# Linear attention into a two-of-eight expert layer: the issue order written out by hand, numerator and denominator in one matmul, one expert begun early, rows transposed on TensorE

## The chip, the cores and the metric

The kernel runs on one core of a Trainium2 chip. The metric is the device time of one execution in microseconds. A core has a matrix engine (TensorE, PE in the profile, with its weight loads as PEld), a vector engine (VectorE, DVE), an activation engine (ScalarE, ACT), GpSimd (POOL), which here issues casting and indirect DMAs, and a sync engine (SP), which issues plain and transposing DMAs.

## The reference, cut to what matters

```python
def phi(x): return np.where(x > 0, x, np.exp(x) - 1.0) + 1.0
q_p, k_p = phi(q), phi(k)                    # 8 batches, 8 heads, 576 tokens, 64
kv  = np.einsum('bhsd,bhse->bhde', k_p, v)
z   = np.sum(k_p, axis=2)
x   = einsum(q_p, kv) / (einsum(q_p, z) + 1e-06)    # as 4608 tokens x 512
noisy = x @ w_gate + np.log1p(np.exp(x @ w_noise)) * noise
top2, top2_w = the two largest of 8, and the softmax of these two
for e in range(8):                           # w1: 512 x 1024, w2: 1024 x 512
    out[mask] += top2_w * (np.maximum(x[mask] @ w1[e], 0) @ w2[e])
```

## The kernel before, in words

**Attention** (class PhaseA) goes through four groups of two batches, 1152 tokens each. GpSimd loads q, k and v with a cast to bf16 (`load`). `phi` is one Exp on ScalarE and a max-add and a min on VectorE. `kv` multiplies keys with values; four extra heads of the value tile are all ones, so the key sums come out of the same matmul. It also multiplies the key-value product with the router weights (`wblk`), which gives 32 router columns beside the 128 numerator and 2 denominator columns of `kvbd`. `q_t` transposes phi(q) on TensorE. `group` then makes, for each three chunks of 128 tokens, the denominators and router columns (tile dl) in matmuls of 34 columns, and the numerators (tile num) in matmuls of 128 columns, and divides on VectorE into the row buffer xr. There are two row buffers, by turns of the group.

**Routing** (`route`) sums the router columns over heads, finds the top two experts, ranks every token within its expert with matmuls of triangular ones, and writes gate data into the row. Then 18 indirect DMAs a group (L358) scatter the rows of 1152 bytes into the DRAM array x_sorted, at the token's place among its expert's rows.

**Experts** (class PhaseB): every expert takes its first 1280 rows (CAP), in blocks of 512, 512 and 256. A transposing DMA (L496) brings a block as xt; `mm1` makes eight tiles of h, with Relu on ScalarE; `mm2` makes y for each 128 rows. The first visit of a token writes y, the second adds to what is there: `gather` brings the older output row into L by an indirect DMA (L438; skipped for first visits by an index out of bounds), VectorE forms gate times y plus L (L464), and an indirect DMA scatters it to the output (L465). The tails of one block (`mm2` and after) stand between the `mm1` parts of the next. Gathers depend on all earlier scatters to the output, since tokens of another expert may be the same. Rows beyond the capacity would be done by `overflow`, a loop at the end; with these inputs no expert has more than 1185 rows.

The framework's scheduler decides the order of instructions on each engine, from the dependencies and the order of the program. Rounds, by which experts could begin before attention ends (`early`), are there but the list ROUNDS is empty, so all experts begin after the last dispatch.

Of the kernel before, what the change touches and what calls it, by code (L numbers as in the profile page):

```python
# [15 lines left out]
P = 128  # L16
# [5 lines left out]

T_CAP = 10
CAP = T_CAP * P
E1 = 3

UNITS = [(0, 0, 9), (1, 0, 9), (2, 0, 9), (3, 0, 9)]

ROUNDS = []
# [3 lines left out]
KVW = 162  # L33
ACT_SET = "natural_log_exp_and_others"
# [11 lines left out]
def build_constants(tc, consts, w_gate, w_noise, noise):  # L46
    nc = tc.nc
    c = {}
    nc.scalar.preload_act_table_set(ACT_SET)

    ident = consts.tile([P, P], BF16, name="ident")
    nc.gpsimd.memset(ident[:], 0.0)
    nc.gpsimd.affine_select(
        out=ident[:], in_=ident[:], compare_op=ALU.not_equal, fill=1.0,
        base=0, pattern=[[-1, P]], channel_multiplier=1,
    )
    c["ident"] = ident

    ut = consts.tile([P, P], BF16, name="ut")
    nc.gpsimd.memset(ut[:], 0.0)  # L60
    nc.gpsimd.affine_select(
        out=ut[:], in_=ut[:], compare_op=ALU.is_ge, fill=1.0,
        base=0, pattern=[[-1, P]], channel_multiplier=1,
    )
    c["ut"] = ut

    ones = consts.tile([P, P], BF16, name="ones")
    nc.vector.memset(ones[:], 1.0)
    c["ones"] = ones


    c8 = consts.tile([P, E], FP32, name="c8")
    nc.gpsimd.iota(c8[:], pattern=[[-1, E]], base=E, channel_multiplier=0,
                   allow_small_or_imprecise_dtypes=True)
    nc.vector.tensor_scalar(out=c8[:], in0=c8[:], scalar1=1.0 / E, scalar2=None, op0=ALU.mult)
    c["c8"] = c8


    tokid = consts.tile([P, 9], FP32, name="tokid")
    nc.gpsimd.iota(tokid[:], pattern=[[1, 9]], base=0, channel_multiplier=9,  # L80
                   allow_small_or_imprecise_dtypes=True)
    c["tokid"] = tokid

    rowpos = consts.tile([P, T_CAP], FP32, name="rowpos")
    nc.gpsimd.iota(rowpos[:], pattern=[[P, T_CAP]], base=0, channel_multiplier=1,
                   allow_small_or_imprecise_dtypes=True)
    c["rowpos"] = rowpos

    mask = consts.tile([P, 130], FP32, name="mask")
    nc.vector.memset(mask[:], 0.0)  # L90
    nc.vector.memset(mask[0:64, 0:64], 1.0)
    nc.vector.memset(mask[0:64, 128:129], 1.0)
    nc.vector.memset(mask[64:P, 64:128], 1.0)
    nc.vector.memset(mask[64:P, 129:130], 1.0)
    c["mask"] = mask


    wst = consts.tile([P, 4, 16], FP32, name="wst")
    for half in range(2):
        for i, w in enumerate((w_gate, w_noise)):  # L100
            nc.scalar.dma_start(
                out=wst[64 * half : 64 * half + 64, :, 8 * i : 8 * i + 8],
                in_=w[256 * half : 256 * half + 256, :].rearrange("(a p) e -> p a e", p=64),
            )
    wblk = consts.tile([P, 4, 32], BF16, name="wblk")
    nc.vector.memset(wblk[:], 0.0)
    nc.vector.tensor_copy(out=wblk[0:64, :, 0:16], in_=wst[0:64])
    nc.vector.tensor_copy(out=wblk[64:P, :, 16:32], in_=wst[64:P])
    c["wblk"] = wblk

    noise_sb = consts.tile([P, 4, 9, E], FP32, name="noise_sb")
    for g in range(4):
        nc.scalar.dma_start(
            out=noise_sb[:, g], in_=noise[g * 2 * S : (g + 1) * 2 * S, :].rearrange("(p c) e -> p c e", c=9))
    c["noise"] = noise_sb

    carry = consts.tile([P, E], FP32, name="carry")
    nc.vector.memset(carry[:], 0.0)
    c["carry"] = carry
    c["cnt"] = [consts.tile([P, E], FP32, name=f"cnt{i}") for i in range(len(ROUNDS))]  # L120
    zero = consts.tile([P, 1], FP32, name="zero")
    nc.vector.memset(zero[:], 0.0)
    c["zero"] = zero
    return c


class PhaseA:


    def __init__(self, ctx, tc, q, k, v, x_sorted, c, psum):  # L130
        self.tc, self.nc, self.c = tc, tc.nc, c
        self.q, self.k, self.v, self.x_sorted = q, k, v, x_sorted
        self.ps_num, self.ps_dl, self.ps_misc = psum
        nc = tc.nc
        pool = lambda name, bufs: ctx.enter_context(tc.tile_pool(name=name, bufs=bufs, side="right"))
        self.kq = pool("A_kq", 3)
        self.pers = pool("A_pers", 1)
        self.ep = pool("A_e", 2)
        self.kvp = pool("A_kvp", 2)
        self.kvt = pool("A_kvt", 1)  # L140
        self.pq = pool("A_pq", 4)
        self.rt = pool("A_rt", 1)
        self.vt, self.xr = [], []
        for i in range(2):
            t = self.pers.tile([P, 12, S], BF16, name=f"v{i}")
            nc.vector.memset(t[:, 8:12, :], 1.0)
            self.vt.append(t)
        for i in range(2):
            t = self.pers.tile([P, 9, ROW_W], BF16, name=f"xr{i}")
            nc.vector.memset(t[:, :, HD:ROW_W], 0.0)  # L150
            self.xr.append(t)
        self.st = {}

    def load(self, g):
        nc = self.nc
        st = {}
        for t in "kvq":
            x = self.vt[g % 2] if t == "v" else self.kq.tile([P, 8, S], BF16, name="kq")
            for j in range(2):
                self.last_load = nc.gpsimd.dma_start(  # L160
                    out=x[64 * j : 64 * j + 64, 0:8, :],
                    in_=getattr(self, t)[2 * g + j].rearrange("h (p c) d -> p h (c d)", c=9)).ins
            st[t] = x
        self.st[g] = st

    def phi(self, x):

        nc = self.nc
        e = self.ep.tile([P, 4, 9, P], BF16, name="e")
        ev = lambda two: e[:, :, :, 64 * two : 64 * two + 64]  # L170
        xv = lambda two: x[:, 4 * two : 4 * two + 4, :].rearrange("p h (c d) -> p h c d", d=D)
        for two in range(2):
            nc.scalar.activation(out=ev(two), in_=xv(two), func=ACT.Exp)  # L173
        flat = x[:].rearrange("p a b -> p (a b)")
        nc.vector.tensor_scalar(out=flat, in0=flat, scalar1=0.0, scalar2=1.0, op0=ALU.max, op1=ALU.add)
        for two in range(2):
            nc.vector.tensor_tensor(out=ev(two), in0=ev(two), in1=xv(two), op=ALU.min)  # L177
        return e

    def kv(self, g, phk):  # L180
        nc, c = self.nc, self.c
        vt = self.vt[g % 2]
        kvbd = self.kvp.tile([P, 2, 4, KVW], BF16, name="kvbd")
        for h in range(2):
            ps = [self.ps_misc.tile([P, 2, 256], FP32, name="misc") for _ in range(2)]
            for i in range(2):
                hp = 2 * h + i
                for ci in range(9):
                    for j in range(2):
                        half = slice(64 * j, 64 * j + 64)  # L190
                        nc.tensor.matmul(  # L191
                            out=ps[j][:, i, 0:192], lhsT=phk[half, hp, ci, :],
                            rhs=vt[half, hp::4, 64 * ci : 64 * ci + 64],
                            start=(i == 0 and ci == 0), stop=(i == 1 and ci == 8), skip_group_check=True,
                        )
            for j in range(2):
                nc.vector.tensor_tensor(
                    out=kvbd[:, j, 2 * h : 2 * h + 2, 0:130], in0=ps[j][:, :, 0:130],
                    in1=_ap(c["mask"], [[0, 2], [1, 130]]), op=ALU.mult,
                )  # L200
        tp = self.ps_misc.tile([P, 1024], BF16, name="misc")
        for i in range(8):
            nc.tensor.transpose(tp[:, i * P : i * P + P], kvbd[:, i // 4, i % 4, 0:128], c["ident"][:])
        kvt = self.kvt.tile([P, 1024], BF16, name="kvt")
        nc.scalar.copy(out=kvt[:], in_=tp[:])
        wp = self.ps_misc.tile([P, 512], FP32, name="misc")
        for i in range(8):
            nc.tensor.matmul(
                out=wp[:, 32 * i : 32 * i + 32], lhsT=kvt[:, i * P : i * P + P], rhs=c["wblk"][:, i % 4, :],
                start=(i == 0), stop=(i == 7), skip_group_check=True,  # L210
            )
        nc.scalar.copy(out=_ap(kvbd, [[KVW, 8], [1, 32]], off=130), in_=wp[:, 0:256].rearrange("p (a b) -> p a b", a=8))  # L212
        return kvbd

    def q_t(self, phq, cs):

        nc = self.nc
        n = len(cs)
        pqt = self.pq.tile([P, 2, 4, P], BF16, name="pqt")
        tp = self.ps_misc.tile([P, 1024], BF16, name="misc")  # L220
        for i, ci in enumerate(cs):
            for hp in range(4):
# [148 lines left out]
class PhaseB:  # L371
# [35 lines left out]
    def meta(self, rows, nt, n_e, rowpos, code, group=None):  # L407
# [6 lines left out]
        if group:  # L414
            self.tc.add_to_no_dep_group(group, r.ins)
# [254 lines left out]
```

## Time and profile before

| | |
|---|---|
| time, median of 3 | 630.37 us (629.78 to 642.35) |
| span of the profiled run | 630.0 us, 6653 instructions |
| busy: PE / DVE / ACT / POOL | 376.8 / 204.0 / 162.1 / 265.9 us |
| matmuls of mm1 / mm2 | 768 / 640 |
| indirect DMAs: dispatch / gather / scatter | 72 / 70 / 80 |
| mean granted TensorE clock | 0.781 |

The span is what ends last; busy times of engines overlap. "Idle before, releaser" tells how long an engine stood still ahead of an instruction and what let it go on. The granted clock is the share of full speed that TensorE got.

### The profile page before, as it was taken

Reading aid. Unit: us, or ns where it says so; the run is one execution under the profiler, and the core shown is the slowest. Engines: PE = TensorE matmul, PEld = TensorE weight load, DVE = VectorE, ACT = ScalarE, POOL = GpSimd, SP = SyncE. Lnnn points to the kernel's source line nnn. Section 1 sums busy time; section 2 is a strip of 40 time slices with the busy share of each in tenths; the row PEclk is TensorE's granted clock in tenths of the full one; section 3 lists DMA queues with packets and bytes.
Section 4 is the critical chain, followed back from the end, with each engine's and each line's share of the span. In section 5 each row is a group of like instructions: output and inputs, shape, how many; then the busy total and the mean of one; then the engine's idle time right before and its main releaser. Section 6 shows DMA issues by size and latency. Waiting matters only on the chain. (4 is left out here: it accounts for less than half of the span.)

```text
span 630.0 us, 6653 instructions
## 1 busy us (share of the span) xinstructions
PE 376.8 (60%) x2520; PEld 204.8 (33%) x2520; DVE 204.0 (32%) x449; ACT 162.1 (26%) x257; POOL 265.9 (42%) x289
## 2 busy tenths in 40 slices
PE   0363634522441004493888997979979969789740
PEld 0352523412331001142334443443444434434410
DVE  4577447563027020021113333223432331333110
ACT  3460620710020002130322431422313314223200
POOL 5220683363720761043225454445445554443541
PEclk9975655755555556697779998997999989979985
DMA  9999939971310369979983443354354543554420
GB/s 147 207 218 249 225 109 195 210 198 53 117 48 1 119 117 199 201 129 184 118 104 111 125 111 116 84 123 125 75 138 141 147 109 101 157 150 119 133 88 18
DMA packets 97034, 83.77 MB, mean 133 GB/s; under 512 B 60469, under 2 KB 82997, under 8 KB 96992
## 3 DMA queue, kind: packets, MB, share of 16 engines
q0 software_dynamic: 40928, 69.90, 48.4%
q1 hardware_dynamic: 54400, 13.18, 13.4%
q10 hardware_dynamic: 1664, 0.18, 0.3%
q8 instruction: 21, 0.34, 0.2%
q14 instruction: 21, 0.17, 0.1%
HBM read 80.72 MB, written 33.95 MB: 182 GB/s over the span
## 5 line engine op out<-in xcount | busy, mean ns | idle before, releaser
L450 PE MATMUL h_ps<-xt,w 128*128 128x512 bf16 (+1 forms) x768 | 159.1, 355 | 67.8 <-DMA xt<-x_sorted 67.8
L458 PE MATMUL y_ps<-w,hT 128*128 128x512 bf16 x640 | 167.1, 409 | 33.2 <-DVE y L464 33.0
L452 ACT ACTIVATE hT<-h_ps 128x512 bf16<-128x512 f32 (+1 forms) x192 | 100.9, 526 | 299.4 <-PE h_ps L450 285.3
L465 POOL DMA_INDIRECT out_dram<-y,si x80 | 79.6, 996 | 123.1 <-DVE y L462 46.4
L450 PEld LDWEIGHTS <-w 128*128 128x128 bf16 x768 | 76.9, 100 | 144.6 <-issue 65.5
L358 POOL DMA_INDIRECT x_sorted<-xr,posi x72 | 72.8, 1011 | 84.0 <-issue 51.4
L464 DVE SCALAR_TENSOR_TENSOR y<-y_ps,gate,L 128x512 f32<-128x512 f32 x70 | 51.5, 737 | 173.3 <-DMA L<-out_dram,gi 108.5
L438 POOL DMA_INDIRECT L<-out_dram,gi x70 | 71.4, 1020 | 85.2 <-DMA out_dram<-y,si 66.5
L458 PEld LDWEIGHTS <-hT 128*128 128x128 bf16 x640 | 66.5, 104 | 115.5 <-issue 55.5
L435 DVE MEMSET L<- 128x512 f32 x70 | 34.0, 485 | 34.2 <-DMA x_sorted<-xr,posi 24.5
L173 ACT ACTIVATE e<-kq 128x2304 bf16<-128x2304 bf16 x16 | 33.5, 2122 | 27.6 <-PE misc L191 8.6
L191 PE MATMUL misc<-v,e 64*128 64x192 bf16 x288 | 24.4, 330 | 21.6 <-DVE e L177 19.9
L240 PE MATMUL num<-kvbd,pqt 128*64 128x128 bf16 x288 | 20.4, 283 | 26.4 <-DVE xr L259 25.9
L240 PEld LDWEIGHTS <-pqt 128*64 128x64 bf16 x576 | 21.8, 144 | 42.3 <-DVE xr L259 24.5
L191 PEld LDWEIGHTS <-e 64*128 64x128 bf16 x288 | 20.7, 123 | 24.1 <-DVE e L177 19.9
L309 PE MATMUL misc<-A,ut 128*128 128x72 bf16 x4 | 0.9, 217 | 44.6 <-DVE A L305 44.6
L259 DVE TENSOR_TENSOR xr<-num,rden 128x512 bf16<-128x512 f32 x36 | 23.5, 686 | 2.7 <-PE num L240 1.8
L225 ACT COPY pqt<-misc 128x1024 bf16<-128x1024 bf16 (+1 forms) x20 | 17.9, 932 | 17.2 <-remote 8.5
L224 PE MATMUL misc<-ident,e 128*128 128x128 bf16 x144 | 16.5, 291 | 9.7 <-ACT kvbd L212 4.5
L177 DVE TENSOR_TENSOR e<-e,kq 128x2304 bf16<-128x2304 bf16 x16 | 21.3, 1342 | 0.1
L403 POOL DMA_DIRECT2D w<-in_moe_w_dram x16 | 12.3, 778 | 17.4 <-DMA kq<-in_k_dram 8.3
L462 DVE TENSOR_SCALAR y<-y_ps,gate 128x512 f32<-128x512 f32 x10 | 7.3, 749 | 32.9 <-PE y_ps L458 28.6
(90 smaller groups left out, 157.8 us busy)
## 6 DMA issues: line engine op xcount, KB each, us to landing
w<-in_moe_w_dram POOLq DMA_DIRECT2D x32, 512.0 KB
kq<-in_k_dram POOLq DMA_DIRECT2D x8, 576.0 KB
v<-in_v_dram POOLq DMA_DIRECT2D x8, 576.0 KB
kq<-in_q_dram POOLq DMA_DIRECT2D x8, 576.0 KB
x_sorted<-zrow SPq DMA_DIRECT2D x16, 144.0 KB
out_dram<-y,si POOLq DMA_INDIRECT x80
x_sorted<-xr,posi POOLq DMA_INDIRECT x72
L<-out_dram,gi POOLq DMA_INDIRECT x70
```

The lines of the kernel that those rows point to most:

```text
L173: nc.scalar.activation(out=ev(two), in_=xv(two), func=ACT.Exp)
L191: nc.tensor.matmul(out=ps[j][:, i, 0:192], lhsT=phk[half, hp, ci, :], rhs=vt[half, hp::4, 64 * ci : 64 * ci + 64], start=(i == 0 and ci == ...
L240: nc.tensor.matmul(out=out[half], lhsT=pqt[ci][:, hp, half], rhs=kvbd[:, j, hp, cols], start=start, stop=stop, skip_group_check=True)
L259: nc.vector.tensor_tensor(out=_ap(xr[:, ci, 0:HD], [[64, 4], [256, 2], [1, 64]]), in0=_ap(ps, [[128, 4], [64, 2], [1, 64]]), in1=_ap(rden[ ...
L358: r = nc.gpsimd.indirect_dma_start(out=self.x_sorted, out_offset=bass.IndirectOffsetOnAxis(ap=posi[:, ci - c0, sl : sl + 1], axis=0), in_= ...
L435: nc.vector.memset(L[:], 0.0)
L438: nc.gpsimd.indirect_dma_start(out=L[:].bitcast(INT32), out_offset=None, in_=self.out.bitcast(INT32), in_offset=bass.IndirectOffsetOnAxis( ...
L450: nc.tensor.matmul(out=ps[:, 0:n], lhsT=w1[:, dc, fc * P : fc * P + P], rhs=xt[:, dc, 0:n], start=(dc == 0), stop=(dc == 3))
L452: nc.scalar.activation(out=hT[:, fc, 0:n], in_=ps[:, 0:n], func=ACT.Relu)
L458: nc.tensor.matmul(out=ps[:], lhsT=hT[:, fc, t * P : t * P + P], rhs=w2[:, fc, :], start=(fc == 0), stop=(fc == 7))
L464: nc.vector.scalar_tensor_tensor(out=y[:], in0=ps[:], scalar=gate, in1=L[:], op0=ALU.mult, op1=ALU.add)
L465: r = nc.gpsimd.indirect_dma_start(out=self.out, out_offset=bass.IndirectOffsetOnAxis(ap=si, axis=0), in_=y[:], in_offset=None, bounds_che ...
```

## The change

Nearly every function is rewritten; what is computed stays. Its parts:

- The scheduler is switched off (`manual_schedule`), and the order on all engines is that of the program. `attention` writes it out: in each of three loop turns the tail of group g is woven with the loads, phi and key-value product of group g + 1, and routing and dispatch of g come at the turn's end. The last group is routed and dispatched in two units of 6 and 3 chunks.
- Numerator, denominator and router columns come out of one matmul of 162 columns (`num`), into a tile of four PSUM banks with one buffer. The ones heads for the key sums are as before. The sum over heads is a tree of three adds.
- CAP is 1216, so blocks have 512, 512 and 192 rows.
- Expert 0 is begun early: its first 512 rows (dispatched after two groups) and next 256 (after three) are done while the last group is routed and dispatched.
- Rows of experts 1 to 7 are loaded untransposed and transposed on TensorE, with a copy on ScalarE (`xn_load`, `xn_t`). Only three blocks of expert 0 use the transposing DMA.
- Gathers and scatters of one expert are declared free of each other (group own). Each indirect DMA has a no-op on GpSimd ahead of it. L has 8 buffers and y has 8.
- `interval` orders a block: at a new expert the old expert's tails (t) come early and the gather at its end; within an expert the gather comes first. T is half of the next block's transposes.
- Weights of experts 0 and 1 are loaded during attention, those of e + 2 at the first block of e.

```diff
-T_CAP = 10
-CAP = T_CAP * P
-E1 = 3
-UNITS = [(0, 0, 9), (1, 0, 9), (2, 0, 9), (3, 0, 9)]
-ROUNDS = []
+CAP = 1216
+T_CAP = 10
+UNITS = [(0, 0, 9), (1, 0, 9), (2, 0, 9), (3, 0, 6), (3, 6, 9)]
+ROUNDS = [(1, 512), (2, 768)]
...
+    def num(self, g, t, *steps):
...
+            self.ps[g, t] = ps = self.ps_num.tile([P, 4, 512], FP32, name="num")
+            for hp in range(4):
+                for i in range(3):
+                    for j in range(2):
+                        half = slice(64 * j, 64 * j + 64)
+                        nc.tensor.matmul(
+                            out=ps[half, hp, KVW * i : KVW * i + KVW], lhsT=self.pqt[g, 3 * t + i][:, hp, half],
+                            rhs=self.kvbd[g][:, j, hp, :], start=(i == 0), stop=(i == 2), skip_group_check=True)
...
-        nc.vector.tensor_reduce(
-            out=lg, in_=_ap(self.lwt[:, c0], [[128, n], [1, 16], [16, 8]]), op=ALU.add, axis=AX.X)
+        for k in (4, 2):
+            nc.vector.tensor_tensor(out=lw(0, k), in0=lw(0, k), in1=lw(k, 2 * k), op=ALU.add)
...
-            r = nc.sync.dma_start(out=xt[:, :, 0:n], in_=self.x_sorted[r0 : r0 + n, 0 : HD // 2].bitcast(BF16),
-                                  transpose=True)
+    def xn_load(self, b):
...
+        nc.sync.dma_start(out=b["xn"][:, 0:k], in_=src(0, k * P).rearrange("(t p) d -> p t d", p=P))
...
+    def xn_t(self, b, h):
...
+            for dc in range(4):
+                nc.tensor.transpose(ps[:, i, dc, 0:m], b["xn"][0:m, t, dc * P : dc * P + P], self.c["ident"][0:m, 0:m])
...
+    def gather(self, b):
...
+            nc.gpsimd.nop()
+            r = nc.gpsimd.indirect_dma_start(
...
+            g = f"own{b['e']}"
+            tc.declare_no_dep(r.ins, group=g, reason="the rows of one expert are of distinct tokens")
+            tc.add_to_no_dep_group(g, r.ins)
...
+    def interval(self, cur, prev, weights=(), nxt=None):
...
+        if new:
+            steps = [0, "t", 1, "t", "t", "t", 2, 3, "T", 4, 5, "T", 6, 7]
         else:
+            steps = [0, 1, "t", 2, 3, "t", "T", 4, 5, "t", "T", 6, 7, "t"]
...
+    for g in range(3):
+        n = g + 1
+        pa.exp(n, "q")
+        pa.num(g, 0, 1)
+        pa.num(g, 1, 0)
+        pa.phi(n, "k")
...
+        if g == 1:
+            pa.dispatch(0, 6, 9)
+            pb.w_tiles(0)
+            pb.w_load(0, 0, 1, 2, 3)
+        pa.kv_mm(n, 0)
+        pa.num(g, 1, 1)
+        pa.num(g, 2, 0)
+        pa.kv_mm(n, 1)
...
+        pa.dispatch(g, 0, 6 if g == 0 else 9)
...
+    pb.mm1(r1, 3, 4, 5, 6, 7)
+    pb.meta("r1", c["cnt"][0][:], col[:, 0:4], code_of(0))
+    pb.interval(r2, r1)
...
+    with ExitStack() as order:
+        order.enter_context(tc.manual_schedule())
...
+        blocks = [pb.block(0, 768, CAP - 768, 0, 6, True)]
+        for e in range(1, E):
+            blocks += [pb.block(e, r, n, e, r // P) for r, n in ((0, 512), (512, 512), (1024, CAP - 1024))]
```

## The prediction

> **What bounds the kernel now.** I read four views. First the page's 40 slices (15.75 us each), for the stages:
>
> ```profile
> PE   0363634522441004493888997979979969789740
> ...
> POOL 5220683363720761043225454445445554443541
> PEclk9975655755555556697779998997999989979985
> DMA  9999939971310369979983443354354543554420
> ```
>
> TensorE is nearly full only from slice 20 (315 us) on. In slices 9 to 13 (142 to 220 us) neither TensorE nor the DMA engines have work. So the first half is bound by an order of waits and not by a resource. The stage table (window; busy us of PE, PEld, DVE, ACT, POOL, each with its count; granted clock; DMA share; GB/s) puts numbers on it:
>
> ```profile
> 0.00:62.00 62.00, 20.00 (x316) 16.87 (x318) 40.30 (x86) 24.72 (x22) 17.10 (x33) 0.79 1.13 204
> 62.00:140.00 78.00, 33.84 (x510) 28.03 (x509) 43.76 (x85) 28.63 (x27) 42.75 (x45) 0.59 0.93 189
> 140.00:227.00 87.00, 20.22 (x288) 16.71 (x288) 23.06 (x86) 7.91 (x16) 40.10 (x42) 0.52 0.21 73
> 227.00:245.00 18.00, 0.07 (x1) 0.07 (x1) 3.33 (x11) 0.00 (x0) 8.08 (x11) 0.50 1.02 155
> 245.00:323.00 78.00, 53.94 (x220) 23.50 (x220) 8.53 (x20) 18.60 (x34) 17.10 (x19) 0.78 1.14 162
> 323.00:365.00 42.00, 39.75 (x193) 19.15 (x192) 13.40 (x29) 13.62 (x26) 20.21 (x21) 0.96 0.41 104
> ```
>
> To 227 us it is attention and dispatch, in which VectorE, the busiest compute engine, works 107 of 227 us. 227 to 245 us TensorE does nothing: all experts wait for the last dispatched row. From 245 us it is experts. The waits (engine, tile, line, releaser: total us, times, longest) name what holds each stage:
>
> ```profile
> DVE y L464 <- DMA L<-out_dram,gi: 108.5, 23, 10.7
> PE h_ps L450 <- DMA xt<-x_sorted: 67.8, 4, 43.7
> POOL L L438 <- DMA out_dram<-y,si: 66.5, 20, 8.2
> PE y_ps L458 <- DVE y L464: 33.0, 12, 5.6
> ACT xr L340 <- DMA x_sorted<-xr,posi: 31.5, 2, 20.7
> ```
>
> The fifth is the stage of 140 us: a small ACT write into the row buffer waits 20.7 us for the dispatch of two groups earlier, and the router's Exp stands behind it. The second is the start of the experts, whose transposing load lands late. The other three are one chain in the expert stage: a gather waits for every earlier scatter, y waits for its gather, TensorE waits for the PSUM of y. The timeline shows the hand-over (start us, length, what):
>
> ```profile
> 225.07 0.96 POOL L358 DMA_INDIRECT x_sorted<-xr,posi  x1 [0.30 <-issue]
> ...
> 228.17 6.11 SPq L496 DMA_TRANSPOSE xt<-x_sorted  x1
> ```
> ```profile
> 244.93 8.53 PE L450 MATMUL h_ps<-xt,w 128*128 128x512 bf16 x32 [43.72 <-DMA xt<-x_sorted]
> ```
>
> In the steady part, 350 to 600 us, the line query counts 571 + 475 matmuls, 1046 in 250 us. An expert has 96 + 80 = 176, so it costs 42.1 us. Last, TensorE ends near 605 and the span at 630: a gather at 609 to 611, y, two scatters, and 13.7 us after the last scatter's issue.
>
> **What the Trainium skill says.** "TensorE: Matmul & The Clock Gate", section What's actually happening: 1.2 GHz when cold, 2.4 GHz after about 3.4 us of activity. The trace agrees: the first matmuls of 512 columns after a wait (from 245.31 us) are 0.43 us apart, later ones 0.216 us. So a TensorE wait costs its length and some 1.7 us more. Same page, Back-to-back issue gap: pairs of weight load and matmul with 128 columns run at about 81 ns; the trace has 16 transposes in 1.30 us at 73.30 us, 81 ns each. (Its 131 ns for 512 columns isn't seen here; I use 0.216.) "DMA: Bandwidth & Descriptors", section SWDGE vs HWDGE vs iDMA: GpSimd's and Sync's DMAs sit in different queues of the same 16 engines, which take turns. That fits the first xt, 16.8 us from issue to use while POOL issued weights.
>
> **The change, part by part.**
>
> *Attention in hand order.* The start to the first numerator stays: k and q land, phi, k'v, transposes; before reaches its first rden at 35.4 us, and I take 41 us, since the one matmul of 162 columns comes after the transposes of the whole group. Then each of three loop turns holds this VectorE work: phi of two tensors 2 x (1.36 + 2 x 1.34) = 8.1; three evacuations of 0.18 + 0.30 + 4 x 0.55 + 2 x 0.33 = 3.3, so 10.0 (the halves estimated from 686 ns for 512 columns and 548 ns for 384); key-value evacuation 4 x 0.42 = 1.7; tree sum in place of the 2.07 us reduce, about 1.4; routing 5.8 (149.25 to 155.0 us). Sum 27. Folding 288 denominator matmuls into the numerator takes 10.5 us of PE busy time away over the kernel, all beside VectorE: nothing on the path. The numerator has a single buffer of four PSUM banks, so TensorE now waits for its evacuation before the next one; on VectorE a phi stands in that gap, which hides it. I take 29 us a turn.
>
> *Dispatch.* 18 scatters at 1.27 us (spacing at 203 to 226 us) are 23 us a group, with loads under 30: below the VectorE turn or level with it. First dispatch at 41 + 29 = 70 us. From there POOL has 72 x 1.27 = 91 and ten issues of loads (the last q, two experts' weights) at 0.70 to 0.78, about 8: 169 us if never kept waiting. The ring does keep it waiting: before needed 116 to 147 us for a group with weight loads between, 8 us more than 23. I add 8, and 3 for landing: 180 us, against 227.
>
> *Early expert.* 768 rows of expert 0 (13.8 + 6.9 us of TensorE at 0.216) run while the last dispatch goes on: hidden by it. What is left waits for rows 768 to 1215 by transposing load: 16.8 us before, beside weights. Here the weights of expert 2 stand behind six scatters, so I take 10; bounds 6 (its issue) and 17. Start 190 us, against 245, and with one load in place of the four waits that drew the next 78 us out.
>
> *Expert work.* 1216 rows for 1280: first matmul 2 x 6.9 + 32 x 0.11 (192 columns, set by the weight load's 0.10) = 17.3; second 80 x 0.216 = 17.3 (the half tile still streams 512 columns); new: 38 transposes at 0.081 = 3.1. Sum 37.7 against 35.0 ideal before (13.8 + 3.9 + 17.3): the rows saved are eaten by transposes, which replace 20 transposing loads that are hidden once things run. The gain must come from the 7 us of waits in 42.1.
>
> *Gathers.* A gather no longer waits for scatters of its own expert, only at the first block of the next, and L has eight buffers in front. There the two tails of the old expert come early: last scatter at about 7 us of the interval, 3 to land (435.07 to 438.22 us), four gathers by 15.5, data 3 later, 18.5. Their y is wanted at 11.7 + 3.5 = 15.2 us. Four PSUM buffers for y hold 7 us of TensorE, so it is covered, narrowly. Behind these gathers stand four weight issues and the next gathers. POOL has 20 x 1.3 + 4 x 0.76 = 29 us an expert, below 37.7; the no-op ahead of each indirect DMA is unseen before: between 0 and 0.3 us (the gap there now); I take 0, the range keeps 6 us an expert, still hidden.
>
> *The sum.* From 190: rest of expert 0, 6.0 + two y tiles 3.5 + transposes 1.3 + cold start 2 = 12.8; its four y tiles 6.9; seven experts 7 x 37.7 = 264; waits 4%, 11 (the y margin is thin). TensorE ends at 485. Tail 16: y 0.75, two scatters, 13.7; no gather in it. **501 us.**
>
> **The rivals.** *Everything fits (12%).* No ring waits, a 6 us load, no waits in the experts: 169 + 3 + 6 + 12.8 + 6.9 + 264 + 15 = 477. For it: POOL and VectorE balance. *Attention is no shorter (15%).* In-order engines with a fixed order: one late wait holds all behind it. In 155 to 180 us the trace shows waits released by "remote", 14.9 and 8.1 us on ACT, long after TensorE's writes, while POOL dispatches; new dispatches lie beside all of attention. Rows at 227: 501 + 47 = 548. Against: before ran its first two groups beside dispatch with little of it. *Experts are no quicker (15%).* Gathers still come late behind weights, in the one GpSimd queue, so 42.1 stays and transposes come on top: 45.2 each, 7 x 7.5 = 52 less the 11: 542. Against: the profile's longest gather waits follow the scatter wait that goes. *POOL becomes the bound (5%).* If the no-op makes each indirect DMA wait for the one before, twice the spacing, 2.5 us each: 70 + 180 + 10 for dispatch, 7 x 53 for experts, 30 for the rest: 661, slower than before. [...] The forecast itself has 53%.
>
> **How the numbers follow.** 501 is the likeliest case. Half of 477's chance lies below 474; 548 is the upper rival. The range 474 to 550 leaves out the POOL case (5%), half of the first rival (6%) and the tails above the other two (7%). Faster by over 2% is below 618, which even both of these together (589) are: all but the POOL case, 95%. That one is slower (3%), or same (2%) where the no-op costs about two thirds of it.
>
> **What would show it.** Right: the last dispatch near 177 us, TensorE full from about 190, experts 37 to 40 us apart, the gather wait of VectorE under 30 us in total, no long wait on xt. Wrong: "remote" or dispatch waits in 70 to 170 us; VectorE waiting for gathers with TensorE cold in between; POOL busy through the expert stage.

## The result, and the profile after

The changed kernel takes **496.0 us** (median of 4, 494.9 to 497.4), the kernel before 630.1 us on the same chip: ratio **0.787, 95% interval 0.784 to 0.790** (medians here and below are over all runs, ratios leave out runs that lie well above the others of their kernel). The forecast was 501 us. These are the slices of the changed kernel's page that answer to those of before; a slice is now 12.3 us:

```profile
PE   0395354554332159999979999999997999999980
DVE  1928999695672102431351351351260342242330
POOL 6121258877667712437568547557467555546550
PEclk9997777666557559999998999999998999999995
DMA  9999993993974345395958846956956955434440
```

TensorE is full from slice 15 (185 us), where before it was slice 20 of 15.8 us (315 us). But look at slices 11 to 13: PE 3, 2, 1 and DVE 7, 2, 1, while POOL stands at 6, 7, 7. There the dispatch goes on and the early expert should run beside it. The stage table (columns as before: window, length, busy us with counts of PE, PEld, DVE, ACT, POOL, granted clock, DMA share, GB/s):

```profile
37.00:66.00 29.00, 14.81 (x209) 12.31 (x206) 25.68 (x69) 18.14 (x19) 4.67 (x7) 0.71 1.21 209
66.00:94.00 28.00, 15.11 (x215) 12.48 (x212) 23.80 (x64) 14.39 (x16) 22.82 (x22) 0.76 0.78 178
94.00:121.00 27.00, 12.75 (x168) 10.56 (x170) 22.62 (x53) 10.41 (x14) 20.60 (x20) 0.67 0.73 163
121.00:152.00 31.00, 12.84 (x111) 8.19 (x112) 20.59 (x89) 5.56 (x17) 21.50 (x24) 0.56 0.81 176
152.00:180.00 28.00, 6.05 (x14) 1.85 (x13) 3.21 (x23) 1.19 (x2) 18.19 (x19) 0.56 0.35 115
180.00:200.00 20.00, 18.08 (x88) 9.19 (x88) 4.13 (x16) 6.44 (x14) 3.92 (x4) 0.87 0.56 138
```

The first three rows are the loop turns, VectorE busy 23 to 26 us of each. In the fifth row (152 to 180 us) ScalarE completes 2 instructions in 28 us and VectorE 23. The timeline of that stretch (start us, length, instruction, in brackets the idle time before it and its releaser):

```profile
150.90 3.42 PE L512 MATMUL b<-xt,w 128*128 128x512 bf16 x8
164.57 1.87 PE L512 MATMUL b<-xt,w 128*128 128x512 bf16 x4 [10.25 <-issue]
175.07 1.86 PE L512 MATMUL b<-xt,w 128*128 128x512 bf16 x4 [8.63 <-issue]
180.70 4.97 PE L512 MATMUL b<-xt,w 128*128 128x512 bf16 x16 [3.77 <-ACT hT L514]
196.82 1.68 PE L512 MATMUL b<-xt,w 128*128 128x448 bf16 x8
...
163.92 0.60 ACT L514 ACTIVATE hT<-b 128x512 bf16<-128x512 f32 x1 [12.55 <-issue]
174.42 0.60 ACT L514 ACTIVATE hT<-b 128x512 bf16<-128x512 f32 x1 [9.90 <-remote]
180.06 1.08 ACT L514 ACTIVATE hT<-b 128x512 bf16<-128x512 f32 x2 [5.04 <-remote]
...
174.72 0.96 POOL L365 DMA_INDIRECT x_sorted<-xr,posi  x1 [0.30 <-issue]
180.51 1.62 SPq L446 DMA_TRANSPOSE xt<-x_sorted  x1
```

Four matmuls run every ten microseconds, and the trace names nothing that was waited for ("issue") or a source that it doesn't know ("remote"). I call this **the stop**. It ends 4 us after the last scatter has been issued; then the rest of the early rows runs, from 180.70 to 196.82 us, and the last rows of expert 0 (448 columns) begin at 196.82, though their load was issued at 180.51. The two names must be read with care. This trace has no landing time for any of the eight kinds of transfer that its page lists; the trace of the same program in the run after_third (below) has one for each. The weights on the two pages, and the same gather in the two timelines, each time the result's run first:

```profile
w<-in_moe_w_dram POOLq DMA_DIRECT2D x32, 512.0 KB
w<-in_moe_w_dram POOLq DMA_DIRECT2D x32, 512.0 KB, 8.5
258.47 1.05 POOL L495 DMA_INDIRECT L<-out_dram,gi  x1 [2.31 <-issue]
246.60 1.05 POOL L495 DMA_INDIRECT L<-out_dram,gi  x1 [2.31 <-DMA out_dram<-y,si]
```

The wait is 2.31 us long in both, and only the second trace names what ended it. So "issue" does not show here that an engine waited for nothing. That the engines stood still is in the start times. The waits that named the stages before:

```profile
DVE y L527 <- DMA L<-out_dram,gi: 14.8, 2, 8.0
POOL L L495 <- DMA out_dram<-y,si: 14.6, 5, 6.2
ACT hT L514 <- remote: 18.2, 5, 9.9
```

The gather wait of VectorE fell from 108.5 to 14.8 us and that of GpSimd's gathers from 66.5 to 14.6; the 67.8 us on xt is gone. (The page of the kernel before has no landing times either, so all these figures may be low; after_third has 18.0 and 18.9, and 22.1 on xt.)

### The profile page after: what moved, and what is told of

Its sections match the earlier page's. It is cut to its first block, busy times and chain, and to the rows that moved or that the text cites. A ratio compares the mean times of both kernels' runs of the same rounds, so it can differ in the third digit from the quotient of the medians.

```text
span 493.9 us, 6809 instructions
## 1 busy us (share of the span) xinstructions
PE 367.1 (74%) x2513; PEld 208.2 (42%) x2513; DVE 209.7 (42%) x526; ACT 187.0 (38%) x304; POOL 269.7 (55%) x289
## 4 chain that ended last, share of the span: by engine, by line
PE 62%; DVE 13%; DMA 10%; issue 4%; another core or an unknown queue 4%; ACT 4%; POOL 1%; POOLq 0%; ACTq 0%
PE b L512 29%; PE b L523 28%; DMA kq<-in_q_dram 7%; PE t L472 3%; DVE xr L254 3%; DMA x_sorted<-xr,posi 2%; DVE e L161 2%; ACT e L151 2%; PE num L243 1%; DVE kq L158 1%; DVE lwt L261 1%; DVE kvbd L192 1%; ACT hT L514 1%; PE misc L227 1%
## 5 line engine op out<-in xcount | busy, mean ns | idle before, releaser
L512 PE MATMUL b<-xt,w 128*128 128x512 bf16 (+3 forms) x768 | 158.1, 350 | 25.6 <-issue 19.3
L514 ACT ACTIVATE hT<-b 128x512 bf16<-128x512 f32 (+3 forms) x192 | 96.0, 510 | 163.2 <-PE b L512 110.4
L523 PE MATMUL b<-w,hT 128*128 128x512 bf16 (+1 forms) x640 | 150.9, 379 | 0.0
L527 DVE SCALAR_TENSOR_TENSOR y<-b,gate,L 128x512 f32<-128x512 f32 x70 | 51.5, 743 | 172.9 <-PE b L523 106.5
L523 PEld LDWEIGHTS <-hT 128*128 128x128 bf16 (+1 forms) x640 | 62.3, 99 | 69.0 <-issue 3.4
L476 ACT COPY xt<-t 128x1024 bf16<-128x1024 bf16 x28 | 28.3, 1011 | 24.9 <-PE t L472 14.9
L243 PE MATMUL num<-kvbd,pqt 128*64 128x162 bf16 x288 | 19.6, 311 | 19.5 <-DVE lwt L261 16.2
L472 PE MATMUL t<-ident,xn 128*128 128x128 bf16 x280 | 21.7, 219 | 6.0 <-ACT xt L476 6.0
L243 PEld LDWEIGHTS <-pqt 128*64 128x64 bf16 x288 | 16.2, 153 | 22.1 <-DVE lwt L261 13.1
L180 PE MATMUL b<-v,e 64*128 64x192 bf16 x144 | 20.0, 314 | 7.0 <-DVE e L161 4.9
L254 DVE TENSOR_TENSOR xr<-num,rden 128x384 bf16<-128x384 f32 x48 | 23.4, 550 | 0.4
```

What stands on the lines that cost most here:

```text
L180: nc.tensor.matmul(out=self.kvps[g, h, j][:, KVM * i : KVM * i + KVM], lhsT=e[half, hp, ci, :], rhs=v[half, hp::4, 64 * ci : 64 * ci + 64] ...
L243: nc.tensor.matmul(out=ps[half, hp, KVW * i : KVW * i + KVW], lhsT=self.pqt[g, 3 * t + i][:, hp, half], rhs=self.kvbd[g][:, j, hp, :], sta ...
L254: nc.vector.tensor_tensor(out=_ap(xr, [[ROW_W, 3], [256, 2], [1, 64]], off=3 * t * ROW_W + 64 * hp), in0=_ap(ps, [[KVW, 3], [64, 2], [1, 6 ...
L472: nc.tensor.transpose(ps[:, i, dc, 0:m], b["xn"][0:m, t, dc * P : dc * P + P], self.c["ident"][0:m, 0:m])
L512: nc.tensor.matmul(out=ps[:, 0:n], lhsT=w1[:, dc, fc * P : fc * P + P], rhs=b["xt"][:, dc, 0:n], start=(dc == 0), stop=(dc == 3))
L514: nc.scalar.activation(out=b["hT"][:, fc, 0:n], in_=ps[:, 0:n], func=ACT.Relu)
```

## The experiments

Three groups of runs, each on one chip, with the kernel before beside it. The groups are rows 1 to 4, 5 to 8 and 9 to 12; after_again and after_third are the changed kernel unedited:

| run | us | before there | ratio to before, 95% |
|---|---|---|---|
| no_early | 501.4 | 613.6 | 0.815 (0.810 to 0.821) |
| paced | 479.3 | 613.6 | 0.779 (0.773 to 0.785) |
| probe | 471.6 | 613.6 | 0.766 (0.760 to 0.773) |
| dma_t | 475.9 | 613.6 | 0.772 (0.765 to 0.779) |
| after_again | 490.2 | 631.5 | 0.773 (0.768 to 0.779) |
| own_off | 533.7 | 631.5 | 0.845 (0.839 to 0.850) |
| sched | 557.7 | 631.5 | 0.882 (0.876 to 0.888) |
| before_own | 607.1 | 631.5 | 0.960 (0.949 to 0.971) |
| after_third | 472.2 | 613.3 | 0.772 (0.768 to 0.777) |
| no_early_2 | 502.2 | 613.3 | 0.820 (0.816 to 0.825) |
| best | 476.7 | 613.3 | 0.780 (0.776 to 0.784) |
| best_paced | 483.5 | 613.3 | 0.790 (0.786 to 0.794) |

The chips differ by 3% in the kernel before, so times are compared within a group.

**Is the early expert hidden?** `no_early` empties ROUNDS and does expert 0 after the dispatch:

```diff
-ROUNDS = [(1, 512), (2, 768)]
+ROUNDS = []
...
-    pb.mm1(r1, 3, 4, 5, 6, 7)
...
-        blocks = [pb.block(0, 768, CAP - 768, 0, 6, True)]
+        blocks = []
-        for e in range(1, E):
+        for e in range(E):
```

> Expert 0 is done whole after the dispatch, in blocks of 512, 512 and 192 rows; nothing of an expert runs beside the dispatch. As the prediction had it (the 768 early rows, 13.8 + 6.9 us of TensorE, are hidden by the dispatch), taking them out costs 16 to 20 us: 512 to 517 us. My theory now: only 6 of the 16 first-matmul chunks of 512 or 256 columns were done beside the dispatch (5 us of TensorE), because all compute engines nearly stop while GpSimd issues scatters one after another; then taking the early expert out costs 3 to 6 us: 499 to 502 us.

501.4 us alone says little, since this chip was faster: the other runs of the group had no stop. So it ran again, and the unedited changed kernel ran on two more occasions, once beside it:

> The changed kernel once more, unedited, beside the kernel before on the chip that this group of runs gets. The first profile of it has a stop in 152 to 180 us and experts of 36.3 to 41.2 us; three other runs with the same dispatch, on another chip, had neither. If the stop belongs to the chip or to the hour, not to the program: where the kernel before runs near 614 us, this runs at 468 to 476 us, ratio 0.763 to 0.775, b0's first matmul is near 183 us and experts are 36.3 us apart; where before runs near 630 us, 494 to 498 us with the stop. If it belongs to this very program (the others' edits moved something): the stop is there again and the ratio is 0.787 wherever it runs.

> The changed kernel unedited, as the measure for the three others on the chip of this group. Two profiles of it have the stop in 152 to 180 us (496 and 494 us), while three kernels with the same dispatch had none on a third chip, where the kernel before took 614 and not 630 us. Theory: it goes with the chip, and shows in the kernel before too. If before is near 614 us here, this is 468 to 476 us with no stop, b0's first matmul near 183 us; if before is near 630 us, 487 to 497 us with the stop. Rival: it goes with the exact program: stop and about 490 us in either case.

> Expert 0 whole after the dispatch, once more, now beside the changed kernel on the same chip. With the stop there: 3 to 8 us slower than the changed kernel, since only 6 of 24 first-matmul chunks were done before the rows were there. Without the stop: 27 to 32 us slower (501 us against some 471), more than the 16 us of the step as predicted, because the first transposing load is then 512 rows long beside the weights and the first block finds TensorE cold.

(Of first-matmul chunks there are 16, not 24.) The changed kernel took 490.2 us where before takes 631.5, 472.2 where it takes 613.3. The profile of after_again has the stop (3 ScalarE instructions in 152 to 180 us), that of after_third has not: the theory of the chip. But after_again missed its number, 494 to 498 us, and its profile is of its longest run, 496.2 us; whether the others, 487.5 to 490.8 us, had the stop in full isn't known. Its ratio, 0.773, isn't the result's 0.787 but that of after_third, 0.772: the kernel before loses there as well. Without the stop, leaving the early expert out costs 502.2 - 472.2 = **30.0 us**. The stage table and TensorE's timeline of after_third show how the step looks when it works:

```profile
152.00:180.00 28.00, 16.68 (x79) 8.08 (x77) 5.92 (x30) 5.58 (x13) 21.19 (x22) 0.87 0.49 135
180.00:200.00 20.00, 17.02 (x85) 8.25 (x86) 4.78 (x13) 7.27 (x12) 5.61 (x7) 0.81 0.71 184
```
```profile
147.92 8.03 PE L512 MATMUL b<-xt,w 128*128 128x512 bf16 x24
159.56 1.31 PE L512 MATMUL b<-xt,w 128*128 128x256 bf16 x8 [3.62 <-DMA xt<-x_sorted]
...
182.98 3.17 PE L512 MATMUL b<-xt,w 128*128 128x448 bf16 x8 [9.46 <-DMA xt<-x_sorted]
```

TensorE works 16.7 us beside the dispatch instead of 6.1, and at 182.98 it waits for rows, not rows for it. In no_early_2 the first matmul of any expert comes later, since its first transposing load takes 512 rows beside the weights:

```profile
195.42 5.89 PE L512 MATMUL b<-xt,w 128*128 128x512 bf16 x16 [56.89 <-DMA xt<-x_sorted]
```

With the stop, leaving the early expert out was not run.

**Does unbroken scatter issue make the stop?** `paced` writes a scratch tile ahead of each of the last 18 scatters, `probe` puts independent writes on VectorE:

```diff
                 self.nc.gpsimd.nop()
+                if u in (3, 4):
+                    self.nc.gpsimd.memset(pad[:], 0.0)
```
```diff
     pa.dispatch(4)
+    pad = pa.rt.tile([P, 320], FP32, name="pad")
+    for i in range(40):
+        pa.nc.vector.memset(pad[:, 8 * i : 8 * i + 8], 0.0)
```

> Ahead of each of the last 18 scatters of the dispatch (units 3 and 4) GpSimd writes a scratch tile of 128 x 512 floats (between 0.4 and 1.0 us, not measured yet), so that these scatters are no longer back to back and the dispatch ends 7 to 18 us later. Theory A, the stop of TensorE, VectorE and ScalarE in 152 to 180 us comes from the unbroken issue of indirect DMAs: the gaps between their instructions shrink to under 1 us, all 16 chunks of the first matmul and the y tiles of expert 0's early rows are done by the last scatter, and the later end of the dispatch is paid back: 490 to 502 us. Rival B, the stop is an ordinary wait (a PSUM buffer, a semaphore behind the router's small operations): the gaps stay, and the time rises by the whole delay: 503 to 514 us.

> 40 tiny writes (128 x 8) to a scratch tile of VectorE, each to its own columns and so independent of each other and of all other work, stand behind the last router operation, in the stopped stretch. Theory A, engines are kept from taking their next instruction while GpSimd issues scatters: the writes come some 0.5 to 2 us apart, with nothing that they could wait for, until the last scatter is issued, and 0.06 to 0.1 us apart from then on. Rival B, waits on other engines: all 40 run 0.06 to 0.1 us apart, 3 to 4 us together. Total time within 3 us of the kernel after in both cases.

Both fell on a chip without the stop and so tell nothing of its cause. The probe's 40 writes took 0.9 us together, as if GpSimd weren't there; the pacing cost 7.7 us against the probe, of which 18 x 0.40 = 7.2 are the wider spacing of the scatters (1.67 for 1.27 us). On a chip with the stop neither was run, so the question stays open.

**Gathers.** `own_off` takes the groups of one expert out of the changed kernel, `before_own` puts them alone into the kernel before:

```diff
         nc.gpsimd.nop()
         r = nc.gpsimd.indirect_dma_start(
...
-        g = f"own{b['e']}"
-        tc.declare_no_dep(r.ins, group=g, reason="the rows of one expert are of distinct tokens")
-        tc.add_to_no_dep_group(g, r.ins)
```

> The groups own0 to own7 are gone: a gather waits again for every scatter issued before it, and a scatter for the gathers, those of its own expert among them. If this wait was the 7 us an expert that the prediction wanted back (waits 42.1 - 35.0), the experts go from 36.3 to 40 to 43 us, 25 to 45 us in total: ratio 0.81 to 0.84. Rival: eight buffers of L and four of y ahead of the wait, and the order in which gathers stand behind the block, hide it: under 8 us, ratio within 0.013 of the kernel after on the same chip.

> The kernel before with one part of the change: its gathers and scatters of one expert are declared free of each other (own0 to own7); nothing else. If the wait of gathers for scatters is what makes its experts 42.1 us rather than 35: 20 to 45 us faster than before, ratio 0.93 to 0.97. Rival: what then ends last is the next wait in the same chain (three and five buffers of L, y's PSUM, the gathers' place behind the block): under 1%, ratio 0.99 to 1.01.

Out: 533.7 - 490.2 = **43.5 us** slower. In, alone: 24 us faster by the medians (the four runs spread from 601.5 to 614.8 us). The waits of own_off show the old chain come back:

```profile
DVE y L524 <- DMA L<-out_dram,gi: 181.4, 36, 12.9
POOL out_dram L534 <- DVE y L524: 57.0, 12, 10.4
POOL L L495 <- DMA out_dram<-y,si: 38.2, 13, 6.3
```

A gather waits for scatters, y for the gather, the next scatter for y. The part is worth more in the new kernel; that a TensorE with fewer other waits has more to lose by this one is my reading, not tested. This chip had the stop, which own_off's ScalarE shows at the same place:

```profile
161.05 0.60 ACT L511 ACTIVATE hT<-b 128x512 bf16<-128x512 f32 x1 [9.99 <-remote]
170.85 0.60 ACT L511 ACTIVATE hT<-b 128x512 bf16<-128x512 f32 x1 [9.20 <-remote]
```

**The written order.** `sched` removes the one line that makes the order binding:

```diff
-        order.enter_context(tc.manual_schedule())
```

> The same program without the region of written order: a scheduler decides the order of each engine's instructions, from its own costs. If the written order makes the attention short: the last dispatch comes at 200 to 230 us and not at 175, 25 us or more above the kernel after, ratio 0.81 or more. Rival: the order is what any scheduler would choose, and the gain is in the numerator, the early expert and the gathers: within 8 us of the kernel after on the same chip.

557.7 us, **67.5 us** slower than the same program in written order. Its last scatter into x_sorted is issued at 201.28 us and not near 175; that is some 27 us. But this chip has the stop, and sched's attention runs into it:

```profile
166.84 0.96 POOL L365 DMA_INDIRECT x_sorted<-xr,posi  x1 [0.30 <-issue]
170.89 0.18 DVE L250 TENSOR_SCALAR rden<-num 128x24 f32<-128x24 f32 x1 [18.40 <-remote]
179.73 0.96 POOL L365 DMA_INDIRECT x_sorted<-xr,posi  x1 [11.93 <-ACT xr L323]
```

The numerators of that rden are issued from 156.43 to 157.47 us, yet VectorE goes on only at 170.89, 3 us after GpSimd has issued the last of 18 scatters in a row; then GpSimd waits 11.93 us for the router. So some 12 of the 27 us (an estimate from these lines) are the stop and not the order by itself. On a chip without the stop sched was not run. The rest of the 67.5 us is lost among the experts, of which the first two take 46.1 and 59.7 us. Their longest wait on VectorE, 18.3 and 25.0 us, is of this kind:

```profile
DVE si L433 <- DMA out_dram<-y,si: 50.1, 6, 25.0
```

The scheduler put the next expert's index operation early into VectorE's queue; it reuses a buffer that scatters still read, and everything behind it waits with it.

**Transposes.** `dma_t` loads every block by transposing load:

```diff
-                pb.xn_load(nb)
+                pb.xt_load(nb)
...
-                if nxt:
-                    self.xn_t(nxt, half)
-                    half += 1
```

> All blocks of the experts are loaded by the transposing load again, and the 38 transposes an expert on TensorE (2.2 us an expert in the trace of after) and their ScalarE copies are gone. If these loads are hidden once things run: 7 x 2.2 = 15 us faster, 481 us. If they come late beside the weights (6 to 17 us each, 21 of them on one queue) or their buffers come free too late, TensorE waits for xt: 496 us or more, with a wait on the transposing load of over 10 us in total.

Neither: ratio 0.772, the same as the changed kernel's on after_third's chip (0.772), and 0.8% above the probe on its own. The 15 us of TensorE are gone, and as much comes back in waits:

```profile
DVE y L527 <- DMA L<-out_dram,gi: 89.8, 18, 10.8
PE b L523 <- DVE y L527: 15.1, 4, 9.5
PE b L512 <- DMA xt<-x_sorted: 23.2, 3, 11.2
```

The wait on xt is the early one that after_third has too (22.1 us). VectorE now waits 89.8 us for gathers, 18.0 there, and TensorE 15.1 us for VectorE's y, where after_third has no such wait. With 34 us of TensorE an expert, the gather chain sets the pace. Whether the gathers themselves are later because more transposing loads run beside them was not tested.

**A better version.** `best` moves expert 1's weights behind the last scatter and gives the row indices a third buffer; `best_paced` adds the pacing:

```diff
-        if g == 1:
-            pb.w_tiles(1)
-            pb.w_load(1, 0, 1, 2, 3)
...
     pa.dispatch(4)
+    pb.w_tiles(1)
+    pb.w_load(1, 0, 1, 2, 3)
...
-... name="posi", bufs=2)
+... name="posi", bufs=3)
```

> Two small edits to the changed kernel for an earlier end of the dispatch: expert 1's four weight loads are issued after the last scatter instead of between the groups 1 and 2 (3.3 us of GpSimd, and ring waits of 1 to 2 us with them), and the row indices get a third buffer, so that the router of unit 3 no longer waits for the scatters of unit 1 (4.3 us on VectorE, 3.4 us of GpSimd standing idle). Dispatch ends 5 to 8 us earlier. Theory: the whole kernel follows, 4 to 8 us faster than the changed kernel on the same chip. Rival: the gain is lost where expert 1's weights now load beside b0's row load and delay it: within 2 us, with a longer wait on xt.

> The kernel 'best' with the scratch write of GpSimd (128 x 512 floats, 0.54 us) ahead of each of the last 18 scatters. On a chip with the stop, theory A (unbroken issue of indirect DMAs on GpSimd keeps the other engines from running): the stop is gone or cut to a half, all of expert 0's early rows are done by the last scatter, 5 to 12 us faster than 'best'. Rival B (not the issue rate): the stop is as before, 4 to 9 us slower than 'best'. On a chip without the stop: 5 to 9 us slower than 'best', the 18 x 0.42 us by which the dispatch ends later.

The rival came true, and more: the last scatter is issued at 166.89 instead of 173.70 us, but the kernel is 4.5 us slower, and none of its four runs is as short as the longest of the changed kernel. The transposing loads of the first early rows and of the last rows of expert 0, in after_third (lines 1 and 2) and in best (from line 3):

```profile
124.51 13.42 SPq L446 DMA_TRANSPOSE xt<-x_sorted  x1
176.71 1.93 SPq L446 DMA_TRANSPOSE xt<-x_sorted  x1
124.38 2.32 SPq L446 DMA_TRANSPOSE xt<-x_sorted  x1
169.32 1.57 POOL L410 DMA_DIRECT2D w<-in_moe_w_dram  x2
169.94 13.48 SPq L446 DMA_TRANSPOSE xt<-x_sorted  x1
187.49 3.17 PE L512 MATMUL b<-xt,w 128*128 128x448 bf16 x8 [22.82 <-DMA xt<-x_sorted]
```

The one load on which all experts wait now shares the DMA engines with 2 MB of weights: its issue takes 13.48 us instead of the 1.93 in after_third. The first load shows the same the other way round: 13.42 us beside expert 1's weights, 2.32 where best has moved them away. "DMA: Bandwidth & Descriptors" in the Trainium skill, section SWDGE vs HWDGE vs iDMA, says that the queues of GpSimd and of the sync engine sit in the same DMA engines, which take turns between them; both pairs of numbers fit. The third index buffer alone, with the weights where they were, was not run. best_paced is 6.8 us slower than best, as expected without the stop, and so tells nothing of it. None of the runs is measurably quicker than the changed kernel. What the single numerator matmul, the smaller CAP and the further buffers are worth by themselves was not run.

## Why the prediction was right

- **Attention in hand order** held: the first rden comes at 37.3 us for 41, and the next groups' at 64.8, 94.1 and 126.9, turns of 27.5, 29.3 and 32.8 us for 29: two held, the third is 3.8 us too long. That the order does it is shown by sched, less what sched lost to the stop.
- **Dispatch** held: first scatter 65.4 us for 70, the last issued at 174.7 for 177, the rows there at 180. Scatters are still 1.27 us apart, so the no-op costs nothing that can be measured, and the rival of POOL as the bound falls.
- **Early expert is the step that failed**: "hidden by it". In the measured run 6 of its 16 chunks were, and 16.1 us came after the rows were there; b0 began at 196.8 us for 190. On a chip without the stop the step is right, and b0 begins at 183.0. The prediction had named the sign, "remote" waits while POOL dispatches, under a rival; it appeared, but beside the last two units and not the attention.
- **Expert work** was mis-sized in two terms: a matmul of 192 columns takes 0.083 us, so 32 of them 2.7 us and not 3.5; a transpose takes 0.056, so 40 take 2.2 us and not 3.1 (the forecast counted 38; and 21 transposing loads went, not 20). The page that I took 81 ns from ("TensorE: Matmul & The Clock Gate" in the Trainium skill, Back-to-back issue gap) has beside it a formula for a single matmul, N / 2.4 + 2.5 ns: 82.5 ns for 192 columns and 55.8 for 128. The full stream here agrees with the formula, and the 81 ns of the trace before come from a stage with a granted clock of 0.59. TensorE's floor is 36 us, not 37.7. The **4% of waits** was put for late y tiles; in the measured run waits like those of the stop fill a part of it: experts are 38.2 us apart on average (forecast 39.3), between 36.3 and 41.6, and 36.3 each in after_third.
- **Gathers** held: "covered, narrowly" is own_off's 43.5 us on one side and dma_t's 89.8 us of waits on the other.
- **The sum** came within 5 us because b0's 6.8 us late start was made good by experts cheaper than forecast; the tail was 15 for 16. This closeness is in part luck: two errors of opposite sign, and a chip with the stop. Without the stop the sum is 29 us too high, and 472.2 us lies below the forecast's range of 474 to 550: there "everything fits", 477 us, was the nearest case.

Between the two profiles of the changed kernel the spans differ by 493.9 - 470.1 = 23.8 us: b0 starts 13.8 us later, 11.6 of it are left at the first of the seven experts, and the next six add 6 x (38.18 - 36.28) = 11.4. So nearly the whole difference lies behind the stop and among the experts. There two experts take 41.0 and 41.6 us; in each TensorE waits for a ScalarE copy (2.71 us before 259.32, 3.29 before 373.29), and the next 16 matmuls take 5.30 and 4.74 us for 3.62 in after_third. That these are short stops of the same kind is my reading.

## What to carry to other kernels

Declare transfers independent where the data are (one expert's rows): a wait of gathers for scatters that write other rows cost 43.5 us here, and 24 in the kernel before. Before moving loads off a queue that is full, ask what they will then run beside: an end 7 us earlier for the dispatch became 4.5 us later for the kernel. Work that is "hidden beside" another engine's is to be checked in the stage's own row, by instructions completed, and on more than one chip.

## What the runs showed of the hardware

In the result's runs and on the chip of the second group, the other engines nearly stop while GpSimd issues indirect DMAs without a break: in 152 to 180 us ScalarE completes 2 instructions and TensorE 14 matmuls, with waits of 9.9 to 12.6 us before single 0.6-us activations, at a DMA share of 0.35. In after_third the same program completes 13 and 79 in that window, and none of the five other profiles from the chips of the first and third group in which an early expert runs there has the stop. The kernel before takes 630 and 631 us where the stop is, 613 and 614 where it is not. Its trace, from the result's chip, has the stop in its own dispatch, whose third group of scatters is issued from 155.78 to 178.29 us:

```profile
167.12 1.01 ACT L205 COPY kvt<-misc 128x1024 bf16<-128x1024 bf16 x1 [14.90 <-remote]
177.33 0.96 POOL L358 DMA_INDIRECT x_sorted<-xr,posi  x1 [0.30 <-issue]
179.83 1.01 ACT L225 COPY pqt<-misc 128x1024 bf16<-128x1024 bf16 x1 [8.05 <-remote]
```

So the stop goes with the chip, or with its state at that hour (the record doesn't name the result's chip), and not with the program: one program has it in the result and in the second group and lacks it in the third. Where it occurs, it keeps to GpSimd's row of scatters wherever that lies: the row ends at 178.3 us in the kernel before, at 167.8 in sched and at 175.7 in the changed kernel, and the others go on 1.5, 3.1 and 4.4 us later. That the unbroken row causes it there is likely from these times, but no run on such a chip took the row apart. Nor can these runs separate the stop from what goes with it: a slower kernel before, and traces without most landing times. A common cause, the recording of the trace among them, is not excluded.
